# One tile by one load, a weight load moved, and the order of two layers in a token-mixing MLP on one Trainium2 core

## The chip, the cores and the metric

The kernel runs on one core of a Trainium2 chip. The metric is the device time of one execution in microseconds. The kernel before took 140.81 us (median of three runs: 141.4, 140.81, 140.53). An engine-by-engine trace of one more execution, the profile, is what everything below is read from.

## What is computed

```python
def reference(x, w1, w2, w3, w4):        # x: 1 x 2048 x 512, w3: 512 x 1792, w4: 1792 x 512, bf16
    h = _gelu(_layernorm(x, axis=-1) @ w1)
    c = D // 4
    g0 = jnp.pad(h[:, :, 0*c:1*c], ((0, 0), (1, 0), (0, 0)))[:, :S, :]
    g1 = jnp.pad(h[:, :, 1*c:2*c], ((0, 0), (0, 1), (0, 0)))[:, 1:, :]
    g2 = jnp.pad(h[:, :, 2*c:3*c], ((0, 0), (2, 0), (0, 0)))[:, :S, :]
    g3 = jnp.pad(h[:, :, 3*c:   ], ((0, 0), (0, 2), (0, 0)))[:, 2:, :]
    hs = jnp.concatenate([g0, g1, g2, g3], axis=-1) @ w2
    x1 = x + hs
    h2 = _gelu(_layernorm(x1, axis=-1) @ w3) @ w4
    return x1 + h2
```

There are two parts. The first normalizes each token, multiplies by w1, applies a gelu, shifts the four quarters of the channels by one or two tokens back or ahead, multiplies by w2 and adds x. The second normalizes again, goes up to 1792 channels through w3 and a gelu, and back through w4.

## The kernel before

The 2048 tokens are 16 tiles of 128, placed so that tile t holds the tokens t, t + 16, t + 32 and so on: a shift by one token is then a neighbouring tile. For each tile VectorE computes row statistics (`stats`, L314) and collects them (`aggr`, L317); the reciprocal root comes from POOL (`rstd_pool`, L338 to L352; for tiles 0 to 3 from ScalarE); the normalized tile `xn` is written by VectorE (`norm`, L367) in the first layer and by ScalarE (L362) in the second. A product needs the tile transposed, with channels on the partitions. This is done in one of two ways: by TensorE against an identity matrix into PSUM (`peT`, L389; `tps` does two tiles) with a copy out by ScalarE (`evacT`, L401; `evs`), or by a DMA that transposes (`dmaT`, L377; `viaDMA` does two tiles), which SP's queue issues. Before the change tiles 0 to 9 of the first layer go over TensorE and tiles 10 to 15 by DMA; all 16 tiles of the second layer go by DMA.

The first product `mm1(p, b)` (L440) treats a pair of tiles into banks from b on, `gelu1(p)` follows on ScalarE (L484 to L501), the second product `mm2` (L515) makes one tile of 128 tokens from the shifted quarters, and `add1` (L527; `adds`) adds x on VectorE. The second products run in the order of tiles 2 to 15, then 0 and 1 (`ORDER2`), because the shifted quarters of tile t come from tiles t − 2 to t + 2. `mm2s(k, b)` and `adds(k)` treat the k-th two of this order. The second layer numbers its tiles q = 16 + k in the same order. `ln2a` makes their statistics and root, `ln2b` the two norms on ScalarE and the two DMA transposes.

The wide layer works in four blocks of 512 tokens: `wide(s)` makes seven steps, each of two chunks of 128 wide channels (`mm3`, L542: eight matmuls; `gelu2`, L555). `narrow(s)` makes the four output tiles of a block (`mm4`, L568: 14 matmuls each; the last add and the store at L582 and L586). `wide(1)` stands before `narrow(0)`, and so on.

Nothing is planned by a program: the body from L606 on is one list of steps, each appended to its engine's queue, and every engine works through its queue in this order. Semaphore waits are derived from who writes and reads each buffer. So the place of a line in the list sets its place behind the other lines of that engine alone. SP's queue holds nearly all DMA issues: the loads of x, w1, w2, w3, then the transposes, and w4 in four pieces between and behind the last transposes. PSUM has 8 banks; `mm1`, `mm2` and `mm3` take them by the number in the call, and wait until the last user of the bank has been read.

Around the change, TensorE's list is: first products of pairs 0 to 3 with transposes of the next pair in the middle of each (tiles 8 and 9 in the middle of pair 3), then pairs 4 to 7, each followed by two tiles of second products, then second products with the first four steps of wide(0) between them:

```python
        mm2s(10, 6), adds(10)
        wide(0, [0, 1])
        ln2a(10), ln2b(10)
        mm2s(12, 4), adds(12)
        wide(0, [2])
```

Of the kernel before, what the change touches and what calls it, by code (L numbers as in the profile page):

```python
# [5 lines left out]
P = 128  # L6
# [151 lines left out]
def bass_standalone__mixer_s_mlp__prompt_kernel(  # L158
# [11 lines left out]
    NT = S // P  # L170
# [10 lines left out]
    x3 = x[0].rearrange("(p t) d -> p t d", t=NT)  # L181
# [3 lines left out]
    with ExitStack() as es:  # L185
        sb = lambda name, shape, dt: es.enter_context(nc.sbuf_tensor(name, shape, dt))
        x_sb = sb("x_sb", [P, NT, D], BF16)
# [7 lines left out]
        w3_sb = sb("w3_sb", [P, DC, F], BF16)  # L195
# [17 lines left out]
        pr = Prog()  # L213
# [4 lines left out]
        g_x = [Gen() for _ in range(NT)]  # L218
# [14 lines left out]
        def bankap(b, n=1):  # L233
            return ps[:, 512 * b : 512 * (b + n)]


        def load_x(eng, t0, n):
            pr.op(eng, f"x{t0}",
                  lambda e: e.dma_start(x_sb[:, t0 : t0 + n, :], x3[:, t0 : t0 + n, :]),
                  w=g_x[t0 : t0 + n], dma=True)  # L240

        def load_x_rows(eng, t, p0, n):
            pr.op(eng, f"x{t}_{p0}",
                  lambda e: e.dma_start(x_sb[p0 : p0 + n, t, :], x3[p0 : p0 + n, t, :]),
                  w=[g_x[t]], dma=True)

        def load_w(name, dst, src, c0=0, n=DC):

            v = src.rearrange("(c p) f -> p c f", p=P)
            pr.op("sp", f"{name}_{c0}",  # L250
                  lambda e: e.dma_start(dst[:, c0 : c0 + n, :], v[:, c0 : c0 + n, :]),
                  w=[g_w[(name, c)] for c in range(c0, c0 + n)], dma=True)

        def all_of(name):
            return [g_w[(name, c)] for c in range(DC)]

        def load_w4(c, n):
            g = Gen()
            g_w4.append(g)
            v = w4.rearrange("(c p) f -> p c f", p=P)  # L260
            pr.op("sp", f"w4_{c}", lambda e: e.dma_start(w4_sb[:, c : c + n, :], v[:, c : c + n, :]),
                  w=[g], dma=True)


        def consts():
            g0 = Gen()
            pr.op("pool", "ident0", lambda e: e.memset(ident[:], 0.0), w=[g0])
            g_ident.prev = g0
            pr.op("pool", "ident1",
                  lambda e: e.affine_select(out=ident[:], in_=ident[:], compare_op=ALU.not_equal,  # L270
                                            fill=1.0, base=0, pattern=[[-1, P]],
                                            channel_multiplier=1),
                  r=[g0], w=[g_ident])
            pr.op("pool", "eps", lambda e: e.memset(eps_c[:], LN_EPS), w=[g_eps])
            pr.op("pool", "nh", lambda e: e.memset(neghalf[:], -0.5), w=[g_nh])
            for (j, i), c in PADS.items():
                pr.op("pool", f"pad{j}{i}",
                      (lambda jj, cc: lambda e: e.memset(hT[:, jj, cc : cc + 1], 0.0))(j, c),
                      w=[g_pad[(j, i)]])
# [15 lines left out]
        def window(j, t):  # L295

            s = (-1, 1, -2, 2)[j]
            u = t + s
            if 0 <= u < NT:
                return pos(j, u), [g_h[(j, u // 2)]]  # L300
            v = u % NT
            pads = [g_pad[k] for k in g_pad if k in PADS and k[0] == j]
            return pos(j, v) + (-1 if s < 0 else 1), [g_h[(j, v // 2)]] + pads


        def src(q):
            if q < NT:
                return x_sb[:, q, :], g_x[q]
            t = ORDER2[q - NT]
            return x1_sb[:, t, :], g_x1[t]  # L310

        def stats(q):
            a, g = src(q)
            pr.op("dve", f"st{q}", lambda e: e.bn_stats(st6[:, q, :], a), r=[g], w=[g_st[q]])  # L314

        def aggr(q):
            pr.op("dve", f"ag{q}", lambda e: e.bn_aggr(mv[:, q, :], st6[:, q, :]),  # L317
                  r=[g_st[q]], w=[g_mv[q]])
# [64 lines left out]
        def peT(q, b):  # L383
            g_tp[q] = (bank[b].new(), b)
            dst = ps_bf[:, 1024 * b : 1024 * b + 512]

            def f(e):
                for c in range(DC):
                    ins = e.transpose(dst[:, P * c : P * (c + 1)],  # L389
                                      xn[:, q % NXN, P * c : P * (c + 1)], ident[:])  # L390
                return ins

            pr.op("pe", f"tp{q}", f, r=[g_xn[q], g_ident], w=[g_tp[q][0]])
# [36 lines left out]
        def mm1(p, b, fcs=(0, 1, 2, 3)):  # L430

            if p not in g_y:
                g_y[p] = ([bank[b].new(), bank[b + 1].new()], b)
            gens, _ = g_y[p]

            def f(e):
                for fc in fcs:
                    dst = ps[:, 512 * b + 256 * fc : 512 * b + 256 * (fc + 1)]
                    for dc in range(DC):
                        ins = e.matmul(dst, w1_sb[:, dc, P * fc : P * (fc + 1)],  # L440
                                       xT[:, dc, 256 * p : 256 * (p + 1)],
                                       start=(dc == 0), stop=(dc == DC - 1))
                return ins

            pr.op("pe", f"mm1_{p}_{len(fcs)}", f, r=all_of("w1") + [g_xT[2 * p], g_xT[2 * p + 1]],
                  w=[gens[h] for h in range(2) if any(fc // 2 == h for fc in fcs)])
# [60 lines left out]
        def mm2(t, b, js=(0, 1, 2, 3)):  # L507

            if t not in g_o:
                g_o[t] = (bank[b].new(), b)  # L510
            win = [window(j, t) for j in js]

            def f(e):
                for j, (c, _) in zip(js, win):
                    ins = e.matmul(bankap(b), hT[:, j, c : c + P], w2_sb[:, j, :],  # L515
                                   start=(j == 0), stop=(j == DC - 1))
                return ins

            r = all_of("w2")
            for _, gs in win:  # L520
                r += gs
            pr.op("pe", f"mm2_{t}_{len(js)}", f, r=r, w=[g_o[t][0]])
# [80 lines left out]
            pr.op("pe", "warm", f, w=[g])  # L603


        load_x_rows("sp", 0, 0, P // 2)  # L606
        load_x_rows("act", 0, P // 2, P // 2)
        for t in range(1, 4):
            load_x("sp", t, 1)
        load_w("w1", w1_sb, w1, 0, 2)  # L610
        load_w("w1", w1_sb, w1, 2, 2)
# [2 lines left out]
        load_x("sp", 8, 4)  # L614
        load_x("sp", 12, 4)
        load_w("w2", w2_sb, w2)
        load_w("w3", w3_sb, w3)
        consts()
        act_table(ACT_F.Sqrt)
        keep_warm(12, 3)  # L620
# [2 lines left out]
        def scale(q):  # L623
            aggr(q), aggr(q + 1)
            rstd_pool(q)

        def st(q):
            stats(q), stats(q + 1)

        def norms(q):  # L630
            norm("dve", q), norm("dve", q + 1)

        def tps(q, b):
            peT(q, b), peT(q + 1, b + 1)

        def evs(q):
            evacT("act", q), evacT("act", q + 1)

        def viaDMA(q):
            dmaT(q), dmaT(q + 1)  # L640

        def mm2s(k, b):
            for i in range(2):
                mm2(ORDER2[k + i], b + i)

        def adds(k):
            for i in range(2):
                add1(ORDER2[k + i])

        def ln2a(k):  # L650
            q = NT + k
            stats(q), stats(q + 1), aggr(q), aggr(q + 1)
            rstd_pool(q, True)

        def ln2b(k):
            q = NT + k
            norm("act", q), norm("act", q + 1)
            viaDMA(q)
# [4 lines left out]
        def wide(s, fps=None):  # L663
            nonlocal n3
            for fp in range(FC // 2) if fps is None else fps:
                mm3(s, fp, Y3[n3 % len(Y3)])
                gelu2(s, fp)
                n3 += 1
# [49 lines left out]
        gelu1(2)  # L718
        scale(8)
        st(10)  # L720
        norms(8)
        mm1(3, 2, (0, 1))
        tps(8, 6)
        mm1(3, 2, (2, 3))
        evs(8)
        gelu1(3)
        scale(10)
        st(12)
        norms(10), viaDMA(10)
        scale(12)  # L730
        st(14)
        norms(12), viaDMA(12)
        scale(14)
        mm2(2, 4, (3,)), mm2(3, 5)
        mm1(4, 0)
        gelu1(4)
        adds(0)
        norms(14), viaDMA(14)
        mm2s(2, 6)
        mm1(5, 2)  # L740
        gelu1(5)
        adds(2)
        ln2a(0), ln2b(0)
        mm2s(4, 4)
        mm1(6, 0), gelu1(6)
# [6 lines left out]
        mm2s(8, 4), adds(8)  # L752
        ln2a(8), ln2b(8)
        mm2s(10, 6), adds(10)
        wide(0, [0, 1])
        ln2a(10), ln2b(10)
        mm2s(12, 4), adds(12)
        wide(0, [2])
        load_w4(0, 4)
        ln2a(12), ln2b(12)  # L760
        mm2s(14, 6), adds(14)
        wide(0, [3])
        load_w4(4, 4)
        ln2a(14), ln2b(14)
        load_w4(8, 4)
        load_w4(12, FC - 12)

        Y3 = [4, 0, 2]
# [42 lines left out]
```

## Time and profile before

| | |
|---|---|
| median of three runs | 140.81 us |
| the profiled execution | 140.27 us |
| its span on the core | 138.0 us |
| instructions | 1802 |
| granted TensorE clock | 1.00 |
| second products L515, 61 recorded matmuls | 14.8 us busy |
| first products L440, 112 matmuls | 13.9 us busy |
| TensorE transposes L389, 40 | 3.3 us busy |
| wide layer L542, 219 recorded matmuls | 48.9 us busy |
| narrow layer L568, 234 recorded matmuls | 48.7 us busy |

How to read it: TensorE is PE, VectorE DVE, ScalarE ACT, GpSimd POOL, SyncE SP. A queue name with a q (SPq) is the engine's sequencer while it issues a DMA. Busy time of a matmul overlaps the next matmul's, so sums of durations are larger than the time that passes; the chain of waits gives the time that each piece took of the path. Lines of the timeline give the start, the time, engine, line, operation and the tiles written and read. "Landing" is the time from the start of a DMA's issue to its last byte.

### The profile page before, as it was taken

The page shows a single profiled execution, that of the slowest core. Times are in us where ns is not written, and L with a number is a line of the kernel's source. Part 1 is how long each engine was busy: PE and PEld are TensorE (multiplying, and loading weights), DVE is VectorE, ACT ScalarE, POOL GpSimd, SP SyncE. Part 2 cuts the span into 40 slices and gives each one's busy share as a digit, 9 for nine tenths or more (in the row PEclk, how much of TensorE's full clock was granted, in tenths as well). Part 3 has the DMA queues.
Part 4 walks back from the last instruction along what each step waited for, and adds up shares of the span by engine and source line. Part 5 has one row for each costly group of instructions (what it writes and reads, how often), then busy time and mean ns, then how long its engine had stood idle before and what let it go on. Part 6 is the DMA issues. An engine that isn't in the chain of part 4 may idle for free.

```text
span 138.0 us, 1802 instructions
## 1 busy us (share of the span) xinstructions
PE 131.6 (95%) x694; PEld 66.9 (48%) x706; DVE 50.2 (36%) x116; ACT 56.3 (41%) x71; POOL 16.9 (12%) x58
## 2 busy tenths in 40 slices
PE   7678999999999999999999999999999999999993
PEld 3265876665444444444444444444444444444452
DVE  0899999998958400000223000022300002232222
ACT  4097862496596796554000455400045540000000
POOL 2005342463333300000000000000000000000000
DMA  2899935434445499200111100011110001111111
GB/s 81 270 320 306 405 104 114 78 72 85 70 85 112 104 231 295 95 5 0 38 38 38 38 0 5 0 38 38 38 38 0 5 0 38 38 38 38 38 68 46
DMA packets 19047, 11.90 MB, mean 86 GB/s; under 512 B 12640, under 2 KB 18016, under 8 KB 19040
## 3 DMA queue, kind: packets, MB, share of 16 engines
q1 hardware_dynamic: 18816, 11.70, 30.7%
q10 hardware_dynamic: 224, 0.10, 0.3%
q8 instruction: 5, 0.08, 0.3%
q14 instruction: 2, 0.02, 0.0%
HBM read 6.82 MB, written 2.10 MB: 65 GB/s over the span
## 4 chain that ended last, share of the span: by engine, by line
PE 84%; DVE 10%; DMA 2%; ACT 1%; issue 1%; DVEq 0%
PE ps L568 35%; PE ps L542 35%; PE ps L515 8%; DVE st L314 6%; PE ps L440 5%; DMA x_sb<-in_x_dram 2%; DVE xn L367 1%; DVE x_sb L527 1%; DVE mv L317 1%; PE ps L389 1%; ACT xT L401 1%; ACT sdv L325 0%; DVE o_sb L582 0%; DVE rstd L331 0%; DVEq L134 0%
## 5 line engine op out<-in xcount | busy, mean ns | idle before, releaser
L542 PE MATMUL ps<-x1T,w_sb 128*128 128x512 bf16 x219 | 48.9, 379 | 0.3
L568 PE MATMUL ps<-w_sb,h2T 128*128 128x512 bf16 (+2 forms) x234 | 48.7, 366 | 0.2
L555 ACT ACTIVATE h2T<-ps 128x1024 bf16<-128x1024 f32 x28 | 28.3, 1020 | 39.0 <-PE ps L542 38.9
L582 DVE TENSOR_TENSOR o_sb<-ps,x_sb 128x512 bf16<-128x512 f32 (+2 forms) x17 | 11.2, 660 | 78.5 <-PE ps L568 78.5
L568 PEld LDWEIGHTS ps<-w_sb,h2T 128*128 128x128 bf16 x238 | 22.8, 98 | 25.9
L542 PEld LDWEIGHTS ps<-x1T,w_sb 128*128 128x128 bf16 x224 | 21.9, 98 | 26.4
L314 DVE BATCH_NORM_STATS2 st<-x_sb 128x6 f32<-128x512 bf16 x32 | 20.4, 675 | 3.9 <-DMA x_sb<-in_x_dram 3.9
L515 PE MATMUL ps<-w_sb,hT 128*128 128x512 bf16 x61 | 14.8, 379 | 0.2
L440 PE MATMUL ps<-xT,w_sb 128*128 128x256 bf16 x112 | 13.9, 273 | 0.5 <-ACT xT L401 0.4
L362 ACT ACTIVATE xn<-x_sb,nmr,rstd 128x512 bf16<-128x512 bf16 x16 | 12.0, 808 | 4.5 <-POOL nmr L352 4.5
L440 PEld LDWEIGHTS ps<-xT,w_sb 128*128 128x128 bf16 x112 | 10.7, 98 | 3.3 <-ACT xT L401 1.1
L527 DVE TENSOR_TENSOR x_sb<-ps,x_sb 128x512 bf16<-128x512 f32 x16 | 10.7, 683 | 3.1 <-PE ps L515 3.1
L347 POOL TENSOR_TENSOR rstd<-vpe,neghalf 128x2 f32<-128x2 f32 x14 | 9.9, 707 | 0.5
L515 PEld LDWEIGHTS ps<-w_sb,hT 128*128 128x128 bf16 x64 | 6.3, 98 | 6.3
L501 ACT ACTIVATE hT<-ps 128x1024 bf16<-128x1024 f32 x6 | 6.2, 1026 | 4.3 <-PE ps L440 4.3
L338 POOL TENSOR_SCALAR vpe<-mv 128x2 f32<-128x2 f32 x14 | 3.1, 220 | 28.4 <-DVE mv L317 28.3
L401 ACT ACTIVATE xT<-ps 128x512 bf16<-128x512 bf16 x9 | 4.9, 593 | 3.3 <-PE ps L389 3.3
L367 DVE TENSOR_SCALAR xn<-x_sb,mv,rstd 128x512 bf16<-128x512 bf16 x16 | 5.9, 410 | 0.3
L600 PE MATMUL ps<-const-bfloat16-1.0 128*128 128x512 bf16 x12 | 4.4, 542 | 0.8 <-PEq L796 0.8
L389 PE MATMUL ps<-ident,xn 128*128 128x128 bf16 x40 | 3.3, 220 | 1.4 <-DVE xn L367 1.3
L317 DVE BATCH_NORM_AGGREGATE mv<-st 128x2 f32<-128x6 f32 x32 | 4.5, 170 | 0.0
L389 PEld LDWEIGHTS ps<-ident,xn 128*128 128x128 bf16 x40 | 2.5, 98 | 2.5 <-DVE xn L367 2.2
(21 smaller groups left out, 16.5 us busy)
## 6 DMA issues: line engine op xcount, KB each, us to landing
w_sb<-in_w_dram SPq DMA_DIRECT2D x4, 512.0 KB, 4.7
out_dram<-o_sb SPq DMA_DIRECT2D x15, 128.0 KB, 1.8
w_sb<-in_w_dram SPq DMA_DIRECT2D x1, 1792.0 KB, 13.2
x_sb<-in_x_dram SPq DMA_DIRECT2D x2, 512.0 KB, 7.0
w_sb<-in_w_dram SPq DMA_DIRECT2D x3, 256.0 KB, 4.7
x_sb<-in_x_dram SPq DMA_DIRECT2D x2, 256.0 KB, 5.2
x_sb<-in_x_dram SPq DMA_DIRECT2D x3, 128.0 KB, 2.7
x1T<-xn SPq DMA_TRANSPOSE x16, 2.5
```

What stands on the lines that cost most here:

```text
L314: pr.op("dve", f"st{q}", lambda e: e.bn_stats(st6[:, q, :], a), r=[g], w=[g_st[q]])
L347: lambda e: e.tensor_tensor(rstd[:, q : q + 2], vpe[:, q : q + 2], neghalf[:], ALU.pow),
L362: lambda e: e.activation(xn[:, s, :], a, ACT_F.Identity, bias=nmr[:, q : q + 1], scale=rstd[:, q : q + 1]),
L367: lambda e: e.tensor_scalar(xn[:, s, :], a, mv[:, q, 0:1], rstd[:, q : q + 1], ALU.subtract, ALU.mult),
L389: ins = e.transpose(dst[:, P * c : P * (c + 1)], xn[:, q % NXN, P * c : P * (c + 1)], ident[:])
L440: ins = e.matmul(dst, w1_sb[:, dc, P * fc : P * (fc + 1)], xT[:, dc, 256 * p : 256 * (p + 1)], start=(dc == 0), stop=(dc == DC - 1))
L515: ins = e.matmul(bankap(b), hT[:, j, c : c + P], w2_sb[:, j, :], start=(j == 0), stop=(j == DC - 1))
L527: lambda e: e.tensor_tensor(x1_sb[:, t, :], bankap(b), x_sb[:, t, :], ALU.add),
L542: ins = e.matmul(bankap(b + i), w3_sb[:, dc, P * fc : P * (fc + 1)], x1T[:, dc, 512 * s : 512 * (s + 1)], start=(dc == 0), stop=(dc == DC ...
L555: pr.op("act", f"g2_{s}_{fp}", lambda e: e.activation(o, a, ACT_F.Gelu_apprx_tanh), r=gens, w=[g])
L568: ins = e.matmul(ps[:, 512 * b : 512 * b + n], h2T[:, fc, s % 2, P * i : P * (i + 1)], w4_sb[:, fc, c0 : c0 + n], start=(fc == 0), stop=(f ...
L582: lambda e: e.tensor_tensor(o_sb[:, s, 0:n], ps[:, 512 * b : 512 * b + n], x1_sb[:, t, c0 : c0 + n], ALU.add),
```

## The change

Four edits. Tile 0 of x is loaded by one DMA on SP instead of two halves on SP and ScalarE. Tiles 8 and 9 are transposed by DMA like tiles 10 to 15, and the first product of pair 3 is made in one piece; w3 is loaded behind the last of these transposes instead of behind w2. The second products of tiles 4 and 5 come before the first product of pair 4; the two adds of tiles 2 and 3 stand earlier in the list, at the same place of VectorE's queue. All second products come before the first block of the wide layer. The norms of the last six tiles of the second layer (k = 10 to 15) are made by VectorE, without the shift that ScalarE's form needs, after all adds; the four pieces of w4 keep their places among the last transposes.

```diff
-        def load_x_rows(eng, t, p0, n):
-            pr.op(eng, f"x{t}_{p0}",
-                  lambda e: e.dma_start(x_sb[p0 : p0 + n, t, :], x3[p0 : p0 + n, t, :]),
-                  w=[g_x[t]], dma=True)
-
...
-        load_x_rows("sp", 0, 0, P // 2)
-        load_x_rows("act", 0, P // 2, P // 2)
-        for t in range(1, 4):
+        for t in range(4):
             load_x("sp", t, 1)
...
         load_w("w2", w2_sb, w2)
-        load_w("w3", w3_sb, w3)
...
-        norms(8)
-        mm1(3, 2, (0, 1))
-        tps(8, 6)
-        mm1(3, 2, (2, 3))
-        evs(8)
+        norms(8), viaDMA(8)
+        mm1(3, 2)
         gelu1(3)
         scale(10)
         st(12)
         norms(10), viaDMA(10)
         scale(12)
+        mm2(2, 4, (3,)), mm2(3, 5)
         st(14)
         norms(12), viaDMA(12)
         scale(14)
-        mm2(2, 4, (3,)), mm2(3, 5)
+        adds(0)
+        mm2s(2, 6)
         mm1(4, 0)
         gelu1(4)
-        adds(0)
         norms(14), viaDMA(14)
-        mm2s(2, 6)
+        load_w("w3", w3_sb, w3)
+        adds(2)
         mm1(5, 2)
         gelu1(5)
-        adds(2)
...
         mm2s(10, 6), adds(10)
+        mm2s(12, 4), adds(12)
+        mm2s(14, 6), adds(14)
         wide(0, [0, 1])
-        ln2a(10), ln2b(10)
-        mm2s(12, 4), adds(12)
-        wide(0, [2])
-        load_w4(0, 4)
-        ln2a(12), ln2b(12)
-        mm2s(14, 6), adds(14)
-        wide(0, [3])
-        load_w4(4, 4)
-        ln2a(14), ln2b(14)
-        load_w4(8, 4)
+        for k in (10, 12, 14):
+            q = NT + k
+            stats(q), stats(q + 1), scale(q)
+            norms(q), viaDMA(q)
+            load_w4(2 * (k - 10), 4)
+        wide(0, [2, 3])
         load_w4(12, FC - 12)
```

## The prediction

> **What bounds the kernel now.** I first read the page's busy shares and slices, then the chain of waits in order of time, then the timeline around 6 to 45 us, then the DMA issues and their landings, last the DMA rate by single microseconds.
>
> ```profile
> PE 131.6 (95%) x694; PEld 66.9 (48%) x706; DVE 50.2 (36%) x116; ACT 56.3 (41%) x71; POOL 16.9 (12%) x58
> PE   7678999999999999999999999999999999999993
> PE 84%; DVE 10%; DMA 2%; ACT 1%; issue 1%; DVEq 0%
> ```
>
> TensorE is busy in every slice but the first four and the last. From the chain:
>
> ```profile
> 0.73 3.02 DMA x_sb<-in_x_dram
> ...
> 3.85 1.29 DVE st L314 x2
> ...
> 8.89 1.25 DVE st L314 x2
> ...
> 12.46 1.09 ACT xT L401 x2
> ...
> 16.62 0.87 PE ps L440 x8
> 17.49 0.45 PE ps L389 x8
> 17.94 0.87 PE ps L440 x8
> 18.81 1.08 PE ps L515 x5
> ```
>
> Until 12 us the chain is the first x tile's load and then VectorE's row statistics and norms. From 13.6 us on it is matmul after matmul: the only steps of others are VectorE's adds and statistics at 23.4 to 29.5, during which TensorE worked anyway (the groups put its idle time at 0.2 us before L515, 0.3 before L542 and 0.2 before L568, in all of the span). So behind 13.6 us only two things can move the end: work taken off TensorE, or a wait put onto it. The granted clock is 1.00 in every stretch I asked for.
>
> **Part by part.** Durations are of the one profiled execution: 140.27 us with a span of 138.0, so 2.27 us lie around the span; the median of the three runs is 140.81, 0.54 above it. I sum on the span and add the difference to the median.
>
> *The eight TensorE transposes of tiles 8 and 9 (tps(8)) go.* The chain shows them as 17.49 to 17.94: 0.45 us on TensorE, on the path: −0.45. Their two evictions on ScalarE (0.59 us each, L401) ran beside matmuls; ScalarE gets 1.1 us free: 0.
>
> *Two DMA transposes more on SP.* The row of the six that exist:
>
> ```profile
> 15.75 0.73 DVE L367 TENSOR_SCALAR xn<-x_sb,mv,rstd 128x512 bf16<-128x512 bf16 x2
> 18.29 7.83 SPq L377 DMA_TRANSPOSE xT<-xn  x6
> 27.98 14.67 SPq L377 DMA_TRANSPOSE x1T<-xn  x10
> ```
>
> Each issue holds SP 1.27 us, the next starts 1.31 us after, and it lands 2.5 us (once 3.2) after its issue. Norm 8 is done at 16.16, so I start T8 (the transpose of tile 8) at 16.19, T9 17.50, T11 20.12, T13 22.74, T15 25.36, SP free at 26.63. Landings: T9 20.0, T11 22.6, T13 25.2, T15 27.9. The new TensorE order, with the chain's own lengths (first product of a pair 1.75 us, second products of two tiles 1.73): pair 3 ends 18.36; five matmuls of tiles 2 and 3 to 19.44; tiles 4 and 5 to 21.2 (their wait for gelu1(3), 18.40 + 1.02 = 19.42, is just met); pair 4 at 21.2 against T9 20.0; pair 5 at 22.95 against T11 22.6; tiles 6, 7 to 26.4; pair 6 at 26.4 against T13 25.2; tiles 8, 9; pair 7 at 29.9 against T15 27.9. Every transpose lands before its reader, the closest by 0.35 us. That tile 4 and 5 move ahead of pair 4 is what hides T9; without this cover pair 4 would start at 19.44 and wait 0.6. If every landing were the 3.2 us one, pair 5 would wait 0.35. I take 0, bounds 0 to +0.4.
>
> *w3 moves from 6.4 us to behind T15.* Gone early: 1.8 MB of traffic in 13 to 19 us, on which nothing waited. New: its issue at 26.65 (w2 and w3 together took 1.05 us to issue, so about 0.55), free at 27.2, before T16 is asked for at 27.98. But T16 to T19, the four transposes that the wide layer's first block reads, now stand behind w3's bytes.
>
> ```profile
> w_sb<-in_w_dram SPq DMA_DIRECT2D x1, 1792.0 KB, 13.2
> 14.00:15.00 1.00, 1.00 (x15) 0.94 (x14) 1.00 (x5) 0.56 (x2) 0.28 (x2) 1.00 1.04 421
> 15.00:16.00 1.00, 0.97 (x10) 0.81 (x9) 0.97 (x3) 1.00 (x2) 0.65 (x1) 1.00 1.01 416
> 16.00:17.00 1.00, 0.98 (x7) 0.68 (x7) 1.00 (x5) 0.99 (x1) 0.22 (x1) 1.00 1.00 405
> ```
>
> (The last columns are granted clock, DMA share, GB/s.) While w3 was the last load under way, the engines moved 405 to 421 GB/s. 1.835 MB by 415 is 4.4 us. The first bytes come about 1.5 us after an issue (x: issued 0.73, moving in 2 to 3 us), so 28.15 to 32.6, and up to 1.5 us more for a thin tail such as 17 to 18.5 us shows. A transpose in such a backlog costs about 0.9 us: from 47.0 to 56.1 us the 1.835 MB of w4 and four transposes went in 9.1 us, of which w4 at its own 340 GB/s (52 to 56 us) took 5.4. Four by 0.9 give T19 at about 36.2, 37.7 with the tail. By the other row, w4's whole mix (2.36 MB in 9.1 us), w3 and four transposes take the same 9.1 us or less: 37.3 at the latest.
>
> *The wide layer's first block after all second products.* Same matmuls, other order. Pair 7 ends 31.6, then eight tiles' second products at 1.73 a pair end at 38.5, and wide(0) starts there instead of 35.35. So w3 (32.6 to 34) and T19 (36.2 to 37.7) are covered by 0.8 to 2.3 us: 0; what it costs without this cover is the first rival. The PSUM banks: tiles 14, 15 need adds(8) out of banks 4, 5, tiles 0, 1 adds(10) out of 6, 7. VectorE: adds(8) end 34.2, statistics of 24, 25 (1.6) to 35.8, adds(10) 36.4 and 37.05; TensorE asks for bank 6 at 36.8 and bank 7 at 37.7. Met by 0.4 and 0.65. After wide starts, nothing waits for those adds.
>
> *Six norms on VectorE.* 6 × 0.37 = 2.2 us more there, plus three waits for POOL's root (0.22 + 0.71 and gaps, about 1.1 us each, with the next pair's statistics queued behind): the last norm ends near 49.8 instead of 49.4 on ScalarE. SP follows: T31 52.0, the last w4 issue ends 53.1, lands 57.8; narrow(0) needs it at 62.6. Its own tiles are read by wide(3), at 99. 0. ScalarE is freed of 4.5 us in a stretch where it was not waited for: 0.
>
> *x tile 0 whole.* The halves landed 2.4 us (SP) and 3.0 us (ACT) after issues at 0.72 and 0.73: 3.73 was the start of all. Whole tiles of 128 KB on SP took 2.7 (median of three, issued next). So 3.4 instead of 3.73. The statistics of tile 4 start at 8.89, and its load, issued 3.90 with 4.9 us to landing, is there at 8.80: the 0.35 us is stopped there, 0.05 to 0.1 is left. Bounds: −0.4, if tile 4 also comes earlier by so much, and +0.3, if the whole tile takes the 3.9 us of the last single tile (the first comes to an idle queue, so I take the 2.7 row). I take −0.05.
>
> The Trainium skill speaks for this part: "DMA: Bandwidth & Descriptors", in its rules of thumb, says two transfers to disjoint partition halves are not worth it, one 128-partition transfer should be used. The measured 3.0 against 2.7 us agrees; by the rule alone the sum would keep the whole 0.35 us and give 140.0, but the row of tile 4's load stops it. The same page speaks against moving w3: section "Bandwidth" has HBM bound a load at about 358 GB/s a core. The row shows 405 to 421 for this very load, and the measurement decides; by the page w3 would take 5.1 us, an estimate from its figure, and T19 still come before 38.5.
>
> Sum: −0.45 + 0 + 0 + 0 − 0.05 = −0.5: span 137.5, profiled time 139.8, median 140.3.
>
> **Rivals.** *A, slower: wide(0) waits for T19 behind w3.* It decides from the point where T19 lands after 38.5: w3 would have to take over 38.5 − 0.5 − 3.6 − 28.15 = 6.2 us, that is under 296 GB/s. For it: the loads at 4 to 5 us went at 204, and w4 with transposes at 288 over all; all data use one queue. Against: w3's own 415. At 204, w3 takes 9.0 us, T19 lands at 41.3, a wait of 2.8: 140.8 − 0.5 + 2.8 = 143.1; half of that, 141.7, is as well possible. *B, the transposes of the first layer are late.* Each of pairs 4 to 7 waits as SP's 1.31 us pace slips, say T8 starts 1 us late: pair 4 waits 0 (21.0 against 21.2), pair 5 0.65, pairs 6 and 7 then nothing more. With 3.2 us landings 1.3: 141.6. For it the margin of 0.35; against it six transposes that kept pace. *C, the head gains in full:* tile 4 comes earlier as well, −0.45 − 0.4: 139.95. Against it: the bytes ahead of tile 4 are the same. That the change does not do what it says I don't see: the order is written out by hand.
>
> **How the numbers follow.** My forecast has 0.60, A 0.20, B 0.10, C 0.10. 1% is 1.4 us, about what a measurement of this kernel can tell from no change. The forecast lies within it, B mostly too; A is beyond it in most of its prices (0.17 of 0.20), and B's worst adds 0.03: slower 0.20. Only C with a low set of runs passes 1% on the other side: 0.05. The range: below, C less the 0.3 by which the lowest run lies under the median, 139.6; above, A's lower half, 142.2.
>
> **What would show it.** Right: no TensorE transposes after 15.5 us, T8 issued near 16.2, pair 5 starting without a wait, wide(0) starting near 38.5 with no idle time before its first matmul, w3's rate near 400 GB/s at 28 to 33 us, tile 4's statistics starting as before, near 8.8, with a wait for DMA ahead of them. Wrong: idle time of TensorE at L542 released by a DMA near 38 us (A), at L440 near 23 (B), statistics of tile 4 at 8.5 (C).

## The result and the profile after

| | before | after |
|---|---|---|
| median of nine runs each | 140.81 us | 139.77 us |
| ratio of the runs | | 0.9912, 95% interval 0.9888 to 0.9936 |
| the profiled execution | 140.27 us | 139.52 us |
| its span | 138.0 us | 137.7 us |
| around the span | 2.27 us | 1.82 us |

The kernel became faster by 1.04 us at the median. The forecast was 0.5 us: the direction is right, and half of the size is missing. The first thing to see is that the profiled spans differ by 0.3 us alone. The larger part of what the profiled executions gained, 0.45 us, lies outside the span, in a line of the table that the prediction had carried over as a constant.

The page after, busy shares and slices, then the chain of waits in order of time:

```profile
PE 131.2 (95%) x686; PEld 66.4 (48%) x698; DVE 52.0 (38%) x122; ACT 51.4 (37%) x63; POOL 15.8 (11%) x52
PE   7677999999999999999999999999999999999993
PE 88%; DMA 4%; DVE 2%; SPq 2%; issue 1%; ACT 1%
```

```profile
2.12 0.43 SPq L239
...
3.58 5.15 DMA x_sb<-in_x_dram
...
8.75 1.28 DVE st L309 x2
...
16.52 1.75 PE ps L435 x16
18.27 1.08 PE ps L510 x5
19.35 0.04 issue
19.38 1.90 PE ps L510 x8
21.28 3.49 PE ps L435 x32
...
38.63 4.32 PE ps L537 x20
```

The first product of pair 3 is one piece of 1.75 us without the 0.45 us of transposes in it. Pairs 4 and 5 follow each other (3.49) without a wait for a DMA. The wide layer follows the second products without idle time. But the eight matmuls of tiles 4 and 5 take 1.90 us and not 1.73, after a break of 0.04 us. And the start of the chain is no longer VectorE's work on tiles 0 to 3: it is SP's issues one after another and then one load, that of tiles 4 and 5, which lands just before 8.75.

The transposes and w3 on SP, and the rate (last column, GB/s) while w3 was under way:

```profile
16.10 10.45 SPq L372 DMA_TRANSPOSE xT<-xn  x8
26.59 0.58 SPq L246 DMA_DIRECT2D w_sb<-in_w_dram  x1
27.77 18.14 SPq L372 DMA_TRANSPOSE x1T<-xn  x12
```

```profile
30.00:31.00 1.00, 1.00 (x11) 0.89 (x10) 0.99 (x2) 0.76 (x2) 0.73 (x2) 1.00 1.03 416
31.00:32.00 1.00, 1.00 (x9) 0.69 (x9) 1.00 (x4) 0.24 (x1) 0.00 (x0) 1.00 1.01 398
32.00:33.00 1.00, 0.95 (x5) 0.48 (x5) 0.49 (x2) 1.00 (x4) 0.72 (x3) 1.00 1.01 383
```

T8 went out at 16.10 and w3 at 26.59, against the prediction's 16.19 and 26.65, and while w3 was under way the engines moved 383 to 416 GB/s.

To compare kernels whose starts scatter, I use one stretch of the chain: from the first product of pair 2 (13.60 before, 13.51 after) to the first matmul of the narrow layer (63.14 and 62.80). Their lines in the two chains, before and then after:

```profile
13.60 1.05 PE ps L440 x8
63.14 7.77 PE ps L568 x36
```

```profile
13.51 1.05 PE ps L435 x8
62.80 1.73 PE ps L563 x8
```

TensorE works through nearly all of this stretch, and it is the same to 0.01 us in the profiles of the kernels that share TensorE's order there: 49.54 before, 49.29 after. So the stretch gave 0.25 us, the time around the span 0.48 (its mean over all executions of the kernels with the longer and the shorter one: 2.30 and 1.82), and of 1.04 us some 0.3 is left for the start.

### The profile page after: what moved, and what is told of

Same layout as the page of the kernel before. It is cut to its first block, busy times and chain, and to the rows that moved or that the text cites. A ratio compares the mean times of both kernels' runs of the same rounds, so it can differ in the third digit from the quotient of the medians.

```text
span 137.7 us, 1779 instructions
## 1 busy us (share of the span) xinstructions
PE 131.2 (95%) x686; PEld 66.4 (48%) x698; DVE 52.0 (38%) x122; ACT 51.4 (37%) x63; POOL 15.8 (11%) x52
## 4 chain that ended last, share of the span: by engine, by line
PE 88%; DMA 4%; DVE 2%; SPq 2%; issue 1%; ACT 1%
PE ps L563 35%; PE ps L537 35%; PE ps L510 10%; PE ps L435 8%; DMA x_sb<-in_x_dram 4%; DVE st L309 2%; SPq L239 1%; ACT xT L396 1%; SPq L246 1%; PE ps L384 1%; DVE xn L362 0%; DVE o_sb L577 0%; DVE mv L312 0%
## 5 line engine op out<-in xcount | busy, mean ns | idle before, releaser
L510 PE MATMUL ps<-w_sb,hT 128*128 128x512 bf16 x61 | 14.3, 380 | 0.2
L435 PE MATMUL ps<-xT,w_sb 128*128 128x256 bf16 x112 | 13.6, 273 | 0.5 <-ACT xT L396 0.4
L362 DVE TENSOR_SCALAR xn<-x_sb,mv,rstd 128x512 bf16<-128x512 bf16 x22 | 8.1, 410 | 3.9 <-POOL rstd L342 3.6
L357 ACT ACTIVATE xn<-x_sb,nmr,rstd 128x512 bf16<-128x512 bf16 x10 | 7.5, 809 | 2.6 <-POOL nmr L347 2.6
L396 ACT ACTIVATE xT<-ps 128x512 bf16<-128x512 bf16 x7 | 3.8, 592 | 3.0 <-PE ps L384 3.0
L384 PE MATMUL ps<-ident,xn 128*128 128x128 bf16 x32 | 2.7, 220 | 1.5 <-DVE xn L362 1.5
L384 PEld LDWEIGHTS ps<-ident,xn 128*128 128x128 bf16 x32 | 2.0, 97 | 2.5 <-DVE xn L362 2.2
```

The costliest lines, as they stand in the source:

```text
L357: lambda e: e.activation(xn[:, s, :], a, ACT_F.Identity, bias=nmr[:, q : q + 1], scale=rstd[:, q : q + 1]),
L362: lambda e: e.tensor_scalar(xn[:, s, :], a, mv[:, q, 0:1], rstd[:, q : q + 1], ALU.subtract, ALU.mult),
L435: ins = e.matmul(dst, w1_sb[:, dc, P * fc : P * (fc + 1)], xT[:, dc, 256 * p : 256 * (p + 1)], start=(dc == 0), stop=(dc == DC - 1))
```

## The experiments

**The load of tile 0, done alone and undone.** e1 is before with the whole tile, e2 is after with the halves.

```diff
-        load_x_rows("sp", 0, 0, P // 2)
-        load_x_rows("act", 0, P // 2, P // 2)
-        for t in range(1, 4):
+        for t in range(4):
             load_x("sp", t, 1)
```

> Only edit against before: tile 0 of x by one DMA on SP. Profiles so far: span 138.0 before, 137.7 after, but 2.27 us lie around the span before and 1.82 after. Theory 1 (the load that ScalarE's queue no longer issues at the start is what takes 0.45 us out of the time around the span): span about 137.9 (statistics of tile 4 start 0.10 earlier), 1.8 around it, time 0.5 to 0.6 us under before (ratio near 0.996). Theory 2 (the time around the span only varies from run to run, and whole-tile loading is worth the 0.10 of the chain): 0.1 us, ratio 0.999 to 1.000. Theory 3 (the head gives its full 0.4 us into the chain in a typical run): span down by 0.4, around it unchanged.

> Only edit against after: tile 0 of x in two halves again, on SP and on ScalarE. Theory 1: 2.27 us around the span again, statistics of tile 4 at 8.85, time 0.5 to 0.6 us above after, so near 140.3, ratio to before 0.996. Theory 2: 0.1 us above after, ratio 0.992. Theory 3: span 0.4 above after.

e1: 140.41 us, ratio 0.9967 (0.9935 to 0.9999), 2.24 to 2.34 us around the span in every run. e2: 140.25 us, ratio 0.9957 (0.9927 to 0.9987), 1.76 to 1.87 around it. Theory 1 falls: the time around the span follows neither the halves nor the whole tile. Theory 2 falls as well in its second half: by the means of the runs, e1's span is 138.05 against 138.49 for before on the same chip, 0.44 us less. Theory 3 fits best: the start gives its gain into the chain. e2's mean span, 138.36, lies 0.42 above the 137.93 of after in the result, though these two were not measured side by side. The size is loose, since e1's interval only just leaves out no change, and some 0.1 us of the 0.44 goes with executions at a lower clock: without those that show a mean clock of 0.988 the spans are 138.05 and 138.39. The stretch from pair 2 to the narrow layer is 49.53 in e1 and 49.30 in e2, which are the values of before and of after.

Where the start gains is seen in SP's issues. The timeline of e2's queue (halves) and of e1's (whole):

```profile
0.73 0.58 SPq L244 DMA_DIRECT2D x_sb<-in_x_dram  x1
1.36 1.77 SPq L239 DMA_DIRECT2D x_sb<-in_x_dram  x3
3.17 0.95 SPq L251 DMA_DIRECT2D w_sb<-in_w_dram  x2
4.16 1.89 SPq L239 DMA_DIRECT2D x_sb<-in_x_dram  x4
```

```profile
0.72 1.82 SPq L239 DMA_DIRECT2D x_sb<-in_x_dram  x4
2.58 0.94 SPq L251 DMA_DIRECT2D w_sb<-in_w_dram  x2
3.57 1.89 SPq L239 DMA_DIRECT2D x_sb<-in_x_dram  x4
```

While ScalarE's queue issues its half beside it, SP's first issue takes 0.55 to 0.58 us and its first three single tiles 1.50 to 1.77; alone, it issues four whole tiles in 1.80 to 1.82. The load of tiles 4 and 5, first of the last line in each, goes out at 3.87 to 4.16 in seven profiles with halves, and at 3.55 to 3.58 in six with the whole tile in the same order of loads. Its landing varies from one execution to the next. VectorE's statistics of tile 4 in e2 and in e1:

```profile
9.99 1.29 DVE L314 BATCH_NORM_STATS2 st<-x_sb 128x6 f32<-128x512 bf16 x2 [1.48 <-DMA x_sb<-in_x_dram]
8.94 1.29 DVE L314 BATCH_NORM_STATS2 st<-x_sb 128x6 f32<-128x512 bf16 x2 [0.80 <-DMA x_sb<-in_x_dram]
```

They began at 8.59 to 10.17 with halves and at 8.04 to 8.94 with the whole tile. VectorE waited for this load in four of the seven profiles with halves (0.75 to 1.48 us) and in three of the six with the whole tile (0.30 to 0.80 us). In the others tile 4 was there in time, and what set its statistics was when VectorE could begin with tile 0: at 3.35 to 3.97 with halves and 2.90 to 3.41 with the whole tile. So the whole tile helps on both ways. That before showed 8.85 with no wait in front of it was an early landing of a wide spread, not the place of a wall.

**The parts of the two layers, each alone in before.** e3 has the first layer's part with w3 moved; e4 has the wide layer's place, with the norms still on ScalarE.

```diff
...
+        norms(8), viaDMA(8)
+        mm1(3, 2)
...
+        mm2s(2, 6)
         mm1(4, 0)
...
+        load_w("w3", w3_sb, w3)
...
```

```diff
         mm2s(10, 6), adds(10)
+        mm2s(12, 4), adds(12)
+        mm2s(14, 6), adds(14)
         wide(0, [0, 1])
         ln2a(10), ln2b(10)
-        mm2s(12, 4), adds(12)
...
```

> Against before: only the first layer's part (tiles 8 and 9 by DMA transpose, w3 behind tile 15, tiles 4 and 5 before pair 4); halves of tile 0 and the interleaved wide layer stay. All theories of the chain: -0.45 for the eight transposes and +0.2 for the wait of tiles 4 and 5 for gelu1(3): span -0.25, time near 140.55, ratio 0.998. But wide(0) now stands at 35.1 while T19 lands behind w3 at 36 to 37: if the late place of wide(0) is what hides w3, TensorE waits 1 to 2 us there and the time is 141.5 to 142.5, ratio 1.005 to 1.012. That is what I expect.

> Against before: only the order, all second products ahead of wide(0); the last six norms stay on ScalarE, between the wide steps. If the order itself takes or gives nothing: span and time of before, ratio 0.999 to 1.001. Rival: contiguous second products save TensorE the change between the layers or some waits for the banks, 0.2 us or more, ratio under 0.999.

e3: 142.25 us, ratio 1.0078 (1.0049 to 1.0108). One of its twelve executions took 793.44 us, which nothing here explains; the ratio leaves it out. The chain:

```profile
31.16 1.76 PE ps L440 x16
32.92 0.02 issue
32.95 0.03 ACT hT L484
32.97 0.10 issue
33.08 4.06 DMA x1T<-xn
37.14 0.14 issue
37.28 3.61 PE ps L542 x16
```

This is the prediction's rival A: TensorE sits idle for 0.92 us until T19, which stands behind w3, has landed at 37.14. The stretch is 50.37, 1.08 more than in after. So moving w3 is bought with the later place of wide(0), as the prediction said. No run leaves w3 at its old place with the rest of the change, so what the move itself gains, if anything, stays open. In after T19 was issued at 32.1 and took 6.0 us, landing at 38.1, some 0.35 us before it was wanted: the 36.2 to 37.7 of the prediction was too early. The issues grew behind the load (1.27 us each before; 1.34 and 2.38 for T18 and T19), but T19's began only 0.3 us later than in before; most of the delay lies behind it.

e4: 141.22 us, ratio 1.0007 (0.9976 to 1.0038), stretch 49.54, 2.24 to 2.32 around the span. The order by itself neither takes nor gives anything that can be seen.

**The six norms, with that order.** e8 is e4 with the norms on VectorE.

```diff
...
-        ln2a(10), ln2b(10)
...
+        for k in (10, 12, 14):
+            q = NT + k
+            stats(q), stats(q + 1), scale(q)
+            norms(q), viaDMA(q)
...
```

> Before, with the second layer's part of the change alone: all second products ahead of wide(0), and the last six norms on VectorE. Against e4 it adds the norms only. Theory of the fetch: 1.8 us around the span, the span of before: time 140.3 to 140.4, ratio 0.997. Rival (the norms themselves change the span, by VectorE's three waits of 1.2 us for POOL): span above before's.

e8: 140.59 us, ratio 0.9966 (0.9934 to 0.9998). Its mean span is that of before on the same chip (138.67 and 138.69), its stretch 49.54, and 1.80 to 1.89 us lie around the span where before has 2.24 to 2.34. With the norms on VectorE half a microsecond is gained, all of it outside the span.

**What fetches at the end.** The DMA queues in the last stretch of the profile, from 133 us on, before and then after (packets, MB, share):

```profile
q1 hardware_dynamic: 288, 0.23, 11.5%
q10 hardware_dynamic: 144, 0.03, 2.5%
q14 instruction: 1, 0.01, 0.6%
```

```profile
q1 hardware_dynamic: 288, 0.23, 11.5%
q10 hardware_dynamic: 144, 0.03, 2.5%
```

Before fetches one more piece of program, on queue q14, when everything is done, after 138 us. The kernels with 2.3 us around the span (before, e1, e3, e4) all have this line, those with 1.8 (after, e2, e8) don't. The norms on ScalarE need a shift, which costs POOL two instructions more for each pair (L343, L352), so that POOL has 58 instructions in the first group and 52 in the second; but ScalarE's and VectorE's programs differ as well. e5 and e6 lengthen one program each.

```diff
+        pad_slot = Slot()
+        for i in range(12):
+            pr.op("pool", f"more{i}",
+                  lambda e: e.memset(nmean[:, 26:27], 0.0), w=[pad_slot.new()])
         last_tile()
```

```diff
+        for i in range(12):
+            act_table(ACT_F.Gelu_apprx_tanh)
         last_tile()
```

> After, with 12 memsets of one column more in POOL's queue near the end, where it has nothing to do (their result is not read). In the four runs with 2.25 to 2.3 us around the span (before, e1, e3, e4) queue q14 fetches instructions once more at the very end; in the two with 1.8 (after, e2) it does not. POOL has 58 instructions in the first four, 52 in the other two; ScalarE 69 to 71 against 63. Theory P (POOL's program is what reaches one more fetch): the late fetch is back, 2.25 us around the span, time near 140.2. Theory A (ScalarE's): 1.8, time of after, 139.8. Rival R (chance): 1.8 and no fetch in both this and e6.

> After, with 12 activations of one column more in ScalarE's queue before the last tile's part, where it has nothing to do (their result is not read). Theory A: the late fetch of q14 is back, 2.25 us around the span, time near 140.2. Theory P: 1.8 us around it, time of after, 139.8.

e5: 139.37 us, 1.78 to 1.86 around the span. The third fetch of q14 came back, but at 36 to 38 us, where nothing waits for it. So the time did not do what I had written; the fetch did come back, but not at the end. e6: 139.17 us, 1.80 to 1.83, two fetches as in after. So q14's fetches go with POOL's program, and a longer program of ScalarE doesn't change them. VectorE was left, and the question whether more POOL instructions can take the fetch away from the end of a kernel that has it. The control e13 has POOL's and VectorE's programs of before and all its transposes on TensorE; e14 adds the memsets.

```diff
-            dmaT(q), dmaT(q + 1)
+            tps(q, 6), evs(q)
```

> Before, with every transpose on TensorE (88 more of 0.056 us, at least 4.9 us, and their evictions on ScalarE); a control for the next three. POOL's program is that of before, 58 instructions. Theory P: a fetch of q14 at the end and 2.3 us around the span, as in before, though TensorE's, ScalarE's and SP's programs are others. Rival: another engine's program decides; 1.8.

> e13 with 12 memsets of one column more at the end of POOL's queue (their result is not read). Theory P: no fetch at the end, 1.8 us around the span, 0.45 to 0.5 us less than e13 at the same span: time gained by adding instructions. Rival D (VectorE's program decides, 116 against 122 instructions): as e13.

Both take some 180 us with spans from 177.0 to 185.2, for TensorE's queue now holds transposes that wait for norms; the totals can't be compared to half a microsecond, but the time around the span can. In e13 it is 2.24 to 2.34 in all four runs, in e14 1.80 to 1.87. The queues after 177 us, e13 and then e14:

```profile
q10 hardware_dynamic: 144, 0.03, 1.2%
q14 instruction: 1, 0.01, 0.2%
```

```profile
q1 hardware_dynamic: 288, 0.23, 5.4%
q10 hardware_dynamic: 144, 0.03, 1.2%
```

VectorE has 116 instructions in both. So changing POOL's program alone is enough to move the fetch away from the end, and it takes 0.46 us off the time around the span. e15 and e16 below, with POOL's program of before, have the late fetch again and 2.23 to 2.33 us. That the six POOL instructions fewer are what takes the late fetch out of after is inferred: e8 changes ScalarE's and VectorE's programs with them, and no run adds memsets to before itself, or just six of them to after. Why both a shorter and a longer program lose the late fetch was not found.

**The wait of tiles 4 and 5.** e7 is after with the gelu of pair 3 in two instructions.

```diff
+            elif p == 3:
+                two(1), two(0)
```

> After, with the gelu of pair 3 in two instructions, quarters 1 and 3 first, which are all that tiles 4 and 5 read of it. If the 0.2 us between tile 3's second product and tile 4's (weights waiting for gelu1(3), 0.53 us of idle time before that weight load) is a wait on the path: span 0.15 to 0.2 under after, ratio to before near 0.991. Rival: the next wait (pair 4 for the transpose of tile 9, landing near 20) takes its place: time of after.

The weight loads of after, around the break at 19.35, and the chain of e7:

```profile
18.00 0.85 PEld L510 LDWEIGHTS ps<-w_sb,hT 128*128 128x128 bf16 x5
19.38 0.11 PEld L510 LDWEIGHTS ps<-w_sb,hT 128*128 128x128 bf16 x2 [0.53 <-ACT hT L496]
```

```profile
15.81 1.75 PE ps L435 x16
17.56 2.81 PE ps L512 x13
20.36 3.49 PE ps L435 x32
```

In after the first weight load of tile 4 (the shifted gelu is the stationary operand here) had to wait for gelu1(3), which ended at 19.32. The matmuls stood still for 0.04 us, but the load could no longer run under the matmul in front of it, and the chain of after has 0.2 us more here than that of e7. In e7 the 13 matmuls are one piece, 2.81 instead of 1.08 + 0.04 + 1.90 = 3.02, and the stretch is 49.08, against 49.29 in after and 49.30 in e5 and e6. The time, 139.5 us with ratio 0.9913 (0.988 to 0.9947), does not resolve this against the 139.37 and 139.17 of e5 and e6: the scatter of the start is larger.

**The start in another kernel.** e15 is e13 with the whole tile, e16 is e15 with tiles 4 and 5 loaded before the second half of w1.

> e13 with tile 0 whole. SP's issues at the start 0.40 to 0.43 us each instead of 0.56 to 0.82 for the first two, tile 4's load issued near 3.58 instead of 3.9 to 4.2, its landing and the end earlier by 0.3 to 0.5 on average; no run with a mean clock of 0.988, which the kernels with halves show in one of five runs and those with a whole tile in one of 36. My theory at the prediction: 0.05.

> e15 with the load of tiles 4 and 5 ahead of the second half of w1. If the landing of tile 4 sets the head, as the chains with a DMA up to 8.4 to 10.4 us say: statistics of tile 4 at 8.0 to 8.4 without a wait, 0.3 to 0.6 us less than e15. Rival: w1's second half is late for the products of pair 0, or ScalarE's table load takes its place: no change.

The issue of tile 4's load moved to 3.55 in e15 as expected. The medians, 184.48 and 182.88 us, say little: in e15 the spans fall into groups between 179.6 and 182.4, and the mean clock is 0.925 to 0.934. My expectation of the clock does not carry over to these kernels. In e16's profile tile 4 is there at 8.08, with no wait; but tile 6 is then waited for, 0.64 us, and TensorE for the second half of w1 up to 9.55. The ratios to before, 1.3008 (1.2945 to 1.307) and 1.2953 (1.2902 to 1.3004), overlap: inconclusive. In this one profile what was taken ahead of one reader was taken from the next.

## Why the prediction was right in its direction and half too small

*Right, with size.* The eight transposes: 0.45 us off the path (e7's stretch lies 0.46 us under that of before). The DMA transposes of the first layer: no reader waited. w3's rate: 383 to 416 GB/s against the 405 to 421 that was drawn on. The Trainium skill's 358 GB/s ("DMA: Bandwidth & Descriptors", section "Bandwidth") is again passed by this load. wide(0): forecast 38.5, seen 38.47, without a wait; its order alone gave nothing. Rival A's wait came only in e3, where wide(0) keeps its early place; there it cost 1.08 us.

*Wrong: "2.27 us lie around the span", added to the median as a constant, and with it the sum of "Six norms on VectorE ... 0".* The part counted VectorE's and ScalarE's work and SP's queue, and did not look at what the POOL instructions that vanish, two for each of three pairs, do to POOL's program. The same step fails in "So behind 13.6 us only two things can move the end": there was a third, behind the last instruction. Where the late fetch is gone the runs have 0.48 us less around the span. The profile of before had the line that shows the fetch, after 138 us.

*Wrong: "x tile 0 whole ... I take −0.05".* The words that failed are those against rival C, "the bytes ahead of tile 4 are the same". They are, but their issue is 0.3 to 0.6 us earlier. It was worth 0.44 us in e1, loosely known, and some 0.3 in the result's medians. I had read tile 4's landing from one execution as if it were fixed. The sign that I had named, tile 4's statistics near 8.8 with a wait for DMA, did appear in the profile of after (8.75, 0.30 us), and proved nothing. "So 3.4 instead of 3.73" was read from one execution too: the statistics of tile 0 began at 3.41 in after, but at 2.90 to 3.07 in the five other profiles with the whole tile.

*Wrong: "their wait for gelu1(3), 18.40 + 1.02 = 19.42, is just met".* Here a wait that is met just as the matmul is due still cost the hidden weight load: 0.2 us against the change.

*Mis-sized, but covered: T19 behind w3.* From w3's issue to T19's landing it took 11.5 us, against 9.6 to 11.1 forecast. The 0.9 us for a transpose rest on a rate that was misread: from 52 to 56 us the engines moved 303 GB/s (341 belongs to 54 to 56), and from 47.0 to 56.1 us 254, not 288. Read rightly the row would give 0.8 us and T19 earlier still, so this row does not carry over to w3. The margin was right in sign alone: 0.8 to 2.3 forecast, 0.35 seen.

The sum by these: 0.45 − 0.2 for the stretch, 0.48 at the end, 0.3 at the start, 1.03 of 1.04 us; the 0.3 is the remainder and not a measurement of its own. Rival C's 139.95 lies nearer to the 139.77 measured than the forecast does, but that is partly luck: its start came true, while neither the 0.2 us lost nor the 0.48 us at the end was in it.

## What to carry to other kernels

Compare the profiled execution's time with its span in both kernels before reading the span, and look for instruction fetches in the last microseconds: here a few instructions more or less on an engine that is off the path moved half a microsecond there. When a start ends on the landing of a load, ask when that load was issued, and how far one execution stands for the others, before calling it a wall. For an operand that is loaded as a matmul's weights, ask that it be ready one weight load before its matmul is due.

## What was not expected of the hardware

An issue took longer beside another queue's: SP's first issue of 64 KB took 0.55 to 0.58 us beside ScalarE's, while one of 128 KB took 0.37 to 0.40 us alone. SP's next issue took 0.56 to 0.82 us, against 0.41 to 0.43, though ScalarE's was over by then. Whether the second queue or the half tile does this, no run separates.

The granted clock at the start is not the same in each execution. In e3's profile (each row: length, busy time of PE, PEld, DVE, ACT and POOL, granted clock, DMA share, GB/s):

```profile
6.00:8.00 2.00, 0.75 (x9) 0.51 (x10) 1.94 (x7) 0.98 (x3) 0.00 (x0) 1.00 0.94 288
8.00:10.00 2.00, 2.00 (x14) 1.61 (x15) 1.96 (x6) 1.39 (x2) 0.00 (x0) 0.56 0.96 331
10.00:12.00 2.00, 2.00 (x15) 1.60 (x13) 1.96 (x7) 1.08 (x2) 0.93 (x2) 0.59 0.96 361
```

After a stretch with TensorE busy for 0.75 of 2 us, about half the clock is granted from 8 to 12 us, and the mean over the span is 0.988. The profile of before has 0.72 us in the same two microseconds and a clock of 1.00 in every row, so such a stretch alone does not decide it. Among the kernels with DMA transposes, 24 of 110 executions with halves show that mean and 1 of 36 with the whole tile; those of before that show it take 141.40 us on average, the others 140.78. The Trainium skill ("TensorE: Matmul & The Clock Gate", Part 1) tells of a clock that is halved after an idle window and of a window that runs on its own time, so that the same kernel can meet it or not; the profile agrees with the half, and before meets it in 13 of 63 executions; the window itself no run here shows. That the earlier start is what spares the whole tile this was not tested.

The page "Runtime: NRT & Kernel Launch" (section "Instruction fetch mechanics") of the same skill calls the cost of such a fetch mostly hidden. Within the run that agrees: e5's fetch at 36 to 38 us cost nothing that can be seen. At the end of before it goes with 0.48 us.
